# A two-row rounded pass for the rows 384 of the cosines, and a last step whose four sums end one by one

## The chip, the cores and the metric

The kernel runs on one core of one Trainium2 chip. The metric is the time of one execution on the device, in microseconds (us). Of the kernel before, three runs took 1657.99, 1658.96 and 1658.97 us; their median is 1658.96 us.

## The reference, cut to what matters

```
X = fft(fft(x, axis=1), axis=2).real          # x: 8 x 3072 x 256
h = X.reshape(24576, 256) @ w_in              # w_in: 256 x 2048
g = maximum(h, 0) + alpha * minimum(h, 0)     # alpha: 2048 values
out = g @ w_out                               # w_out: 2048 x 256
```

## The kernel before

The transform over the 256 features is multiplied into `w_in` once, so what is left for each of the 8 batches is a cosine and a sine transform over the 3072 rows. Its input is folded first: rows that meet the same cosine or sine are added or subtracted, which leaves four tiles of at most 6 x 128 rows, `fce`, `fco`, `fse` and `fso` (even and odd, cosine and sine). They are multiplied with the tables `ee`, `eo` and `er` on TensorE (PE) by `dft`, L490 to L511, and the result goes to the tile `X` as a high part (rounded to the short format float32r) and a low part (the rest).

The two matmuls of the network run in 26 blocks of up to 512 columns, with 16 steps of 128 hidden units in each, 416 steps in all. A step is a first matmul (L686 to L688, three rounded passes for each of two outputs `pq`), the activation on VectorE (DVE, L704, L712, L659), ScalarE (ACT, L716 and the high part L665) and GpSimd (POOL, the low part L667), and a second matmul (L769, twelve passes into four sums `acc`). The first matmul runs three steps ahead of the second. Each engine works in the order in which the program is written. The transforms of batch b+1 stand between the steps of batch b: `cee` (even cosines) at step 40 of the batch, and the two odd ones (`unit_odd`) at its own steps 0 and 3.

One row of the folded cosines is left over: 384, with 2688, 1152 and 1920 folded onto it. Its factors are +1 and -1 in turn. In `dft` it is a matmul of its own (`zr` on table row 4) with the tile `zres`, 128 partitions of which only partition 0 isn't zero; its dtype is float32, which PE takes as two records. It belongs to three of the eight transforms of a batch: `cee`, and the `ca` half of both odd ones. `middle` holds high and low parts of the table's middle rows; they exist from batch 1 on, and batch 0 takes its middle rows in float32.

The values of these rows are made for all batches at the start, in `rows_384` on DVE, out of `xres`. One DMA on ACT's queue writes them to `resd` in DRAM (L831). `place_rows_384` (L468, ACT's queue) and `fold_rows` (L434, SyncE's queue, SP) bring them back into partition 0. `fold_128` puts column 128's value beside them on POOL (L421).

At the start eight matmuls on `dummy` run first. The folding of batch 0 is shared: `fold_sums` on PE (L392, pieces 0, 1, 3 and 5) with a copy on ACT (L399, `xeg`) and the rest on DVE (`fold_rest`, L409 to L417), and pieces 2 and 4 on DVE alone (L383). The parts of the weights come from 64-bit words: `weights_f` on ACT (L269 to L271), `weights_b` on DVE (L276, L280), `weights_m` on POOL (L289), then PE (L320).

The DMAs complete on eight semaphores in turn. Before a DMA is issued, its queue waits until the one eight before it has landed.

At the end `evacuate` copies the four sums out (L783, L785) and writes them in two DMAs (L786).

Of the kernel before, what the change touches and what calls it, by code (L numbers as in the profile page):

```python
# [20 lines left out]
P = 128  # L21
# [63 lines left out]
def _tables():  # L85
    p = PI.reshape(3, P)
    j, i2 = np.arange(193)[None, :], np.arange(192)[None, :]

    def four(full):
        a, b = np.zeros_like(full[1]), np.zeros_like(full[1])  # L90
        a[:64], b[64:] = full[1][:64], full[1][64:]
        return np.stack([full[0], a, b, full[2]], 1)

    cee = four([_cos(p[c][:, None] * j, 768) for c in range(3)])
    see = four([_sin(p[c][:, None] * j, 768) for c in range(3)])
    ceo = four([_cos(p[c][:, None] * (2 * i2 + 1), 1536) for c in range(3)])
# [3 lines left out]
    res = np.zeros((P, 1, 193))  # L100
    res[0] = (-1.0) ** np.arange(193)
# [8 lines left out]
    out = dict(  # L110
        ee=np.concatenate([cee, res, see], 1), eo=np.concatenate([ceo, seo], 1),
        er=np.concatenate([rca, res * _cos(384, 3072), rsb], 1), feat=feat, ident=ident,
    )
    return {k: np.ascontiguousarray(v, dtype=np.float32) for k, v in out.items()}

# [18 lines left out]
def fft2_prelu_ffn(ctx: ExitStack, tc: tile.TileContext, t, outputs):  # L134
# [26 lines left out]
    zres = small.tile([P, 3, P], F32, name="zres")  # L161
# [4 lines left out]
    ee = tabs.tile([P, 9, 193], F32, name="ee")  # L166
    eo = tabs.tile([P, 8, 192], F32, name="eo")
    er = tabs.tile([P, 9, 193], F32, name="er")


    wih, wil = wts.tile([P, KF, 2, P], F32R, name="wih"), wts.tile([P, KF, 2, P], F32R, name="wil")
# [4 lines left out]
    x128 = st.tile([P, 28, NB], F32, name="x128")  # L176
    xres = st.tile([P, 4, 2, 8], F32, name="xres")

    resd = dram.tile([P, 4, 8], F32, name="resd")
    xcd = dram.tile([NB, 1544], F32, name="xcd")  # L180


# [46 lines left out]
    S.dma_start(out=ident, in_=t["ident"])  # L229
    S.dma_start(out=xres, in_=t["xres"])  # L230
    S.dma_start(out=consts, in_=t["consts"])
    load(4)

    G.memset(zres, 0.0)
    G.memset(ebias, -896.0 * 2.0**23)
    G.memset(dummy.bitcast(F32), 0.0)

# [180 lines left out]

    def fold_128(b):
        G.tensor_copy(out=fold[b, "so"][:, :, 0:1], in_=f128[:, 6:12, b:b + 1])  # L420
        G.tensor_copy(out=zres[0:1, 2, 0:1], in_=r128[0:1, b:b + 1])  # L421

    def fold_whole(i, e):
        yield from fold_piece(i, e)
# [1 line left out]

    def fold_rows(b):

        places = (zres[0:1, 0], zres[0:1, 1], zres[0:1, 2], fold[b, "se"][0:1, 3])
        places = [v.rearrange("p (c d) -> p c d", d=8) for v in places]  # L430
        for i, v in enumerate(places):
            if b == i == 0:
                continue
            nc.sync.dma_start(  # L434
                out=v, in_=resd[16 * b:16 * b + 16, i].rearrange("(o c) d -> o c d", o=1),
            )

    def turn_rows(b, nm):

# [11 lines left out]
    def rows_384():  # L451

        bufr = st.tile([P, 64, 8], F32, tag="w32", name="bufr", bufs=2)
        xe, xo, a, r = (bufr[:, 4 * i:4 * i + 4] for i in range(4))
        tt = V.tensor_tensor
        tt(out=xe, in0=xres[:, :, 0], in1=xres[:, :, 1], op=ALU.add)
        tt(out=xo, in0=xres[:, :, 0], in1=xres[:, :, 1], op=ALU.subtract)
        x2, o2 = (v.rearrange("p (j i) d -> p j i d", i=2) for v in (xe, xo))
        tt(out=a[:, 0:2], in0=x2[:, :, 0], in1=x2[:, :, 1], op=ALU.add)
        tt(out=a[:, 2:4], in0=o2[:, :, 0], in1=o2[:, :, 1], op=ALU.subtract)  # L460
        tt(out=r[:, 0], in0=a[:, 0], in1=a[:, 1], op=ALU.add)
        tt(out=r[:, 1], in0=a[:, 0], in1=a[:, 1], op=ALU.subtract)
        tt(out=r[:, 2], in0=a[:, 2], in1=a[:, 3], op=ALU.add)
        tt(out=r[:, 3], in0=a[:, 2], in1=a[:, 3], op=ALU.subtract)
        return r

    def place_rows_384():
        S.dma_start(  # L468
            out=zres[0:1, 0].rearrange("p (c d) -> p c d", d=8), in_=resd[0:16, 0].rearrange("(o c) d -> o c d", o=1),
        )  # L470


    TABS = dict(cee=(ee, 0), see=(ee, 5), ceo=(eo, 0), seo=(eo, 4), ca=(er, 0), sb=(er, 5))
    middle = {}

    def parts(key, n, rows, places):
# [13 lines left out]
    def dft(kind, v, zr, m, mid=None, bank=None):  # L490

        ps = (bank or other_bank())[0:m]
        tab, at = TABS[kind]
        n = tab.shape[-1]
        even, odd = [(v[:, 0], tab[:, at])], [(v[:, 2], tab[:, at + 3])]
        if zr is not None:
            even.append((zr, tab[:, 4]))
        if mid is None:
            even.append((v[:, 1], tab[:, at + 1]))
            odd.append((v[:, 1], tab[:, at + 2]))  # L500
        else:
            (fh, fl), (th, tl) = mid, middle[kind]
            for i, (lhsT, rhs) in enumerate(((fh, th), (fh, tl), (fl, th))):
                nc.tensor.matmul(out=_pairs(ps[:, 0:2 * n]), lhsT=lhsT, rhs=_halves(rhs), start=(i == 0), stop=False)  # L504
        for o, terms in ((0, even), (n, odd)):
            for i, (lhsT, rhs) in enumerate(terms):
                nc.tensor.matmul(  # L507
                    out=ps[:, o:o + n], lhsT=lhsT, rhs=rhs, start=(mid is None and i == 0),
                    stop=(i == len(terms) - 1 and (o > 0 or mid is None)),
                )  # L510
        return ps, n, m  # L511
# [79 lines left out]


    f128 = small.tile([P, 12, NB], F32, name="f128")
    z128 = st.tile([P, NB], F32, name="z128")

    def column_128():
        tt = V.tensor_tensor
        buf8 = st.tile([P, 64, NB], F32, tag="w32", name="buf8", bufs=2)
        a = buf8[:, 0:12].rearrange("p (c j) b -> p c j b", c=3)
        ae = buf8[:, 12:18].rearrange("p (c j) b -> p c j b", c=3)  # L600
        ao = buf8[:, 18:24].rearrange("p (c j) b -> p c j b", c=3)
        v = x128[:, 0:24].rearrange("p (c j i) b -> p c j i b", c=3, i=2)
        for c in range(3):
            tt(out=a[:, c], in0=v[:, c, :, 0], in1=v[:, c, :, 1], op=ALU.add)
            a2 = a[:, c].rearrange("p (j i) b -> p j i b", i=2)
            tt(out=ae[:, c], in0=a2[:, :, 0], in1=a2[:, :, 1], op=ALU.add)
# [9 lines left out]
        G.memset(z128, 0.0)  # L616
        tt(out=z128[0:1], in0=r[:, 0], in1=r[:, 1], op=ALU.add)
        tt(out=r128, in0=r[:, 0], in1=r[:, 1], op=ALU.subtract)

    def warm_up(n):  # L620
# [121 lines left out]
    def ffn2(s):  # L742
# [7 lines left out]
        if s < WHOLE:  # L750
# [5 lines left out]
                    )  # L756
            return
        H, L = 0, 1
        if f == KF - 1:
# [15 lines left out]
    def evacuate(g, o):  # L775
# [2 lines left out]
            outs[g] = outp.tile([P, 2, 2, w], F32, tag="o", name="o")  # L778
        v = outs[g]
        dst = outputs[g]  # L780
        for i in range(2):
            if o == 1 and (i == 1 or g < len(BLOCKS) - 1):
# [171 lines left out]


_INS = [
    "xh", "xres", "x128", "w", "consts", "ee", "eo", "er", "feat", "ident",
]


# [57 lines left out]
```

## Time and profile before

| | |
|---|---|
| runs | 1657.99, 1658.96, 1658.97 us |
| profiled execution | 1658.04 us |
| its span, first to last instruction | 1656.3 us |
| PE busy | 1635.3 us, 99% |
| DVE busy | 1495.5 us, 90% |
| POOL busy | 1326.9 us, 80% |
| ACT busy | 1133.1 us, 68% |

Shares over the whole span say little of the first 45 us, in which the kernel loads and folds, and of the last 5 us. Those two stretches, and one step in the middle, are read by themselves.

### The profile page before, as it was taken

How to read it: one execution, taken by the hardware profiler on the slowest of the kernel's cores; microseconds unless marked ns; L12 is line 12 of the kernel's file. 1: busy time of each engine (PE TensorE's matmuls, PEld its weight loads, DVE VectorE, ACT ScalarE, POOL GpSimd, SP SyncE). 2: the span in 40 equal slices, each digit the busy share in tenths (PEclk: the TensorE clock that was granted, in tenths of full speed). 3: DMA queues.
4: the chain of work that ended last, by engine and by line, in shares of the span. 5: the costliest groups of instructions: out<-in, count | busy, mean ns of one | idle time of the engine just before them, and what ended most of it. 6: DMA issues, size and time to landing. Idle time of an engine off the chain costs nothing.

```text
span 1656.3 us, 26300 instructions
## 1 busy us (share of the span) xinstructions
PE 1635.3 (99%) x8154; PEld 1464.1 (88%) x8154; DVE 1495.5 (90%) x2613; ACT 1133.1 (68%) x2095; POOL 1326.9 (80%) x1420
## 2 busy tenths in 40 slices
PE   8999999999999999999999999999999999999998
PEld 6778999888888888888888888888888888899998
DVE  7979998999889997999989998899988999889997
ACT  5866777666676666766676666766667666677675
POOL 2378998888888887889878898888887888776665
PEclk9999999999999999999999999999999999999999
DMA  6410120021000110010200101001110010000000
GB/s 240 141 56 19 45 70 20 7 71 39 33 27 20 58 52 20 33 39 33 70 1 32 51 33 58 27 7 70 39 33 26 20 45 31 1 31 25 25 20 20
DMA packets 25289, 69.93 MB, mean 42 GB/s; under 512 B 6174, under 2 KB 7486, under 8 KB 25150
## 3 DMA queue, kind: packets, MB, share of 16 engines
q1 hardware_dynamic: 24398, 67.80, 11.6%
q8 instruction: 65, 1.06, 0.3%
q14 instruction: 74, 0.61, 0.1%
q10 hardware_dynamic: 752, 0.45, 0.1%
HBM read 42.98 MB, written 25.25 MB: 41 GB/s over the span
## 4 chain that ended last, share of the span: by engine, by line
PE 92%; DVE 3%; POOL 2%; ACT 2%; issue 1%; DMA 0%; ACTq 0%; DVEq 0%; POOLq 0%
PE acc L769 55%; PE pq L686 10%; PE pq L688 9%; PE pq L687 9%; PE ps L507 3%; PE acc L753 2%; PE ps L504 2%; DVE d L712 1%; PE ps L320 1%; POOL lo L667 1%; ACT pq L716 1%; DVE d L659 1%; DVE pf L704 1%; ACT hi L665 0%; PE fold L392 0%
## 5 line engine op out<-in xcount | busy, mean ns | idle before, releaser
L667 POOL TENSOR_TENSOR lo<-d,hi 128x512 fp32r<-128x512 f32 (+2 forms) x804 | 971.9, 1226 | 242.4 <-ACT hi L665 214.8
L665 ACT ACTIVATE hi<-d 128x512 fp32r<-128x512 f32 (+2 forms) x804 | 482.6, 600 | 360.7 <-DVE d L659 282.2
L659 DVE SCALAR_TENSOR_TENSOR d<-d,sg,pq 128x512 f32<-128x512 f32 (+2 forms) x804 | 564.5, 702 | 11.8 <-ACT pq L716 11.7
L716 ACT ACTIVATE pq<-d,sga 128x512 f32<-128x512 f32 (+2 forms) x804 | 526.3, 655 | 47.9 <-DVE d L712 46.3
L712 DVE TENSOR_TENSOR d<-pf,pq 128x512 f32<-128x512 f32 (+2 forms) x832 | 529.6, 640 | 11.1 <-POOL lo L667 3.2
L769 PE MATMUL acc<-hi,woh 128*128 128x512 f32 (+2 forms) x1608 | 456.5, 365 | 1.5 <-ACT o L785 1.4
L769 PE MATMUL acc<-hi,wol 128*128 128x512 f32 (+2 forms) x1608 | 392.9, 364 | 0.0
L769 PE MATMUL acc<-lo,woh 128*128 128x512 f32 (+2 forms) x1608 | 392.9, 364 | 0.0
L704 DVE SCALAR_TENSOR_TENSOR pf<-xbc,w,pq 128x512 f32<-128x512 f32 (+2 forms) x416 | 298.2, 717 | 81.9 <-PE pq L688 75.8
L769 PEld LDWEIGHTS acc<-hi,woh 128*128 128x128 f32 x1608 | 298.0, 189 | 35.7 <-ACT o L785 4.8
L769 PEld LDWEIGHTS acc<-lo,woh 128*128 128x128 f32 x1608 | 295.3, 189 | 30.9
L769 PEld LDWEIGHTS acc<-hi,wol 128*128 128x128 f32 x1608 | 295.3, 189 | 30.8
L686 PE MATMUL pq<-X,wih 128*128 128x512 f32 (+2 forms) x832 | 313.2, 376 | 8.5 <-DVE d L659 7.7
L687 PE MATMUL pq<-X,wih 128*128 128x512 f32 (+2 forms) x832 | 302.4, 364 | 0.3 <-DVE X L590 0.3
L688 PE MATMUL pq<-X,wil 128*128 128x512 f32 (+2 forms) x832 | 302.4, 364 | 0.0
L686 PEld LDWEIGHTS pq<-X,wih 128*128 128x128 f32 x832 | 157.7, 190 | 30.7 <-PE pq L688 5.8
L688 PEld LDWEIGHTS pq<-X,wil 128*128 128x128 f32 x832 | 157.6, 189 | 15.7 <-DVE wil L337 0.3
L687 PEld LDWEIGHTS pq<-X,wih 128*128 128x128 f32 x832 | 157.8, 190 | 15.2 <-issue 0.5
L383 POOL TENSOR_TENSOR raw<-raw 128x512 f32<-128x512 f32 (+2 forms) x84 | 69.4, 827 | 0.0
L289 POOL TENSOR_TENSOR w<-we,wm 128x512 int32<-128x512 int32 x16 | 20.4, 1273 | 51.5 <-DVE wm L280 47.1
L525 DVE TENSOR_TENSOR y<-ps,os 128x193 f32<-128x193 f32 (+3 forms) x68 | 21.1, 352 | 30.9 <-ACT os L515 30.9
L785 ACT ACTIVATE o<-acc 128x512 f32<-128x512 f32 (+2 forms) x53 | 26.9, 557 | 25.6 <-PE acc L769 25.5
(160 smaller groups left out, 1069.7 us busy)
## 6 DMA issues: line engine op xcount, KB each, us to landing
raw<-in_xh SPq DMA_DIRECT2D x46, 512.0 KB
out<-o SPq DMA_DIRECT2D x36, 512.0 KB
raw<-in_w SPq DMA_DIRECT2D x15, 512.0 KB
xbc<-xcd SPq DMA_DIRECT2D x18, 256.0 KB
out<-o SPq DMA_DIRECT2D x10, 386.0 KB
out<-o SPq DMA_DIRECT2D x6, 384.0 KB
before<-in_xh SPq DMA_DIRECT2D x2, 512.0 KB
xbc<-xcd SPq DMA_DIRECT2D x5, 193.0 KB
```

The costliest lines, as they stand in the source:

```text
L383: yield size, lambda o=o, i0=i0, i1=i1, op=op: e.tensor_tensor(out=o, in0=i0, in1=i1, op=op)
L507: nc.tensor.matmul(out=ps[:, o:o + n], lhsT=lhsT, rhs=rhs, start=(mid is None and i == 0), stop=(i == len(terms) - 1 and (o > 0 or mid is ...
L659: V.scalar_tensor_tensor(out=g, in0=d, scalar=sg[:, f:f + 1], in1=ad, op0=ALU.mult, op1=ALU.max)
L665: S.activation(out=hi, in_=d, func=ACTF.Copy)
L667: G.tensor_tensor(out=lo, in0=d, in1=hi.bitcast(F32), op=ALU.subtract)
L686: nc.tensor.matmul(out=out, lhsT=wih[:, f, q], rhs=xh, start=True, stop=False)
L687: nc.tensor.matmul(out=out, lhsT=wih[:, f, q], rhs=xl, start=False, stop=False)
L688: nc.tensor.matmul(out=out, lhsT=wil[:, f, q], rhs=xh, start=False, stop=True)
L704: V.scalar_tensor_tensor(out=_pairs(pf), in0=_halves(xbc[g]), scalar=w128[:, f:f + 1], in1=_pairs(ps[0]), op0=ALU.mult, op1=ALU.add,)
L712: V.tensor_tensor(out=d, in0=pf, in1=ps[1], op=ALU.add if i else ALU.subtract)
L716: S.activation(out=ad, in_=d, func=ACTF.Copy, scale=sga[:, f:f + 1])
L769: nc.tensor.matmul(out=out, lhsT=wt[:, f, o * P:(o + 1) * P], rhs=rhs, start=(f == 0 and n[o] == 0), stop=(f == KF - 1 and n[o] == 2),)
```

## The change

For the left-over row, `rows_384` multiplies in the factor cos(pi/4) of the odd transforms, rounds the three rows on ACT to a high part, takes the low part on DVE, and writes both to DRAM tiles `resph` and `respl`, each with a second small DMA that puts column 128's value into place. `place_rows_384` loads the two as two partitions of `zst` and copies them to `zres`, now 2 partitions of float32r: on ACT for batch 0, on POOL for the others. `dft` multiplies `zres` with `res`, two rows of +1 and -1 and a zero at the end: where `middle` exists as one rounded pass of 194 columns, in batch 0 as before in float32. The tables lose their row 4. The last of the 416 steps orders its twelve passes sum by sum, and the last evacuation copies and stores each sum by itself, the fourth in two halves, on ACT's and SP's queue.

```diff
+        V.tensor_scalar(out=r[:, 1:3], in0=r[:, 1:3], scalar1=COS_384, scalar2=None, op0=ALU.mult)
+        parts = bufr[:, 16:32].bitcast(F32R).rearrange("p (k i) d -> p k i d", k=4)
+        r1 = parts[0:1, 3].rearrange("p i d -> p (i d)")
+        V.tensor_scalar(out=r128, in0=r128, scalar1=COS_384, scalar2=None, op0=ALU.mult)
+        S.activation(out=parts[:, 0, 0:3], in_=r[:, 0:3], func=ACTF.Copy)
+        V.tensor_tensor(out=parts[:, 1, 0:3], in0=r[:, 0:3], in1=parts[:, 0, 0:3].bitcast(F32), op=ALU.subtract)
+        S.activation(out=r1[:, 0:NB], in_=r128, func=ACTF.Copy)
+        V.tensor_tensor(out=r1[:, NB:2 * NB], in0=r128, in1=r1[:, 0:NB].bitcast(F32), op=ALU.subtract)
+        S.dma_start(out=resd, in_=r[:, 3])
+        for i in range(2):
+            S.dma_start(out=resp[i].rearrange("i p d -> p i d"), in_=parts[:, i, 0:3].bitcast(F32))
+            S.dma_start(
+                out=resp[i].rearrange("i (b c) d -> c i b d", c=16)[0:1, 2, :, 0], in_=r1[:, i * NB:(i + 1) * NB].bitcast(F32),
+            )
+
+    def place_rows_384(b, queue):
+        for i in range(2):
+            queue.dma_start(
+                out=zst[i:i + 1], in_=resp[i][:, 16 * b:16 * b + 16].rearrange("(o i) c d -> o i (c d)", o=1),
+            )
+        if b:
+            G.tensor_copy(out=zres, in_=zst)
+        else:
+            S.activation(out=res, in_=rst, func=ACTF.Copy)
+            S.activation(out=zres, in_=zst, func=ACTF.Copy)
...
     def dft(kind, v, zr, m, mid=None, bank=None):
-        if zr is not None:
-            even.append((zr, tab[:, 4]))
         if mid is None:
+            if zr is not None:
+                even.append((zr.bitcast(F32), res[0:zr.shape[0], 0:n].bitcast(F32)))
...
             for i, (lhsT, rhs) in enumerate(((fh, th), (fh, tl), (fl, th))):
+                if i == 2 and zr is not None:
+                    nc.tensor.matmul(out=ps[:, 0:n + 1], lhsT=zr, rhs=res, start=False, stop=False)
...
     def ffn2(s):
+        if s == NSTEP - 1:
+            for o in range(2):
+                for i in range(2):
+                    for n, (wt, part) in enumerate(((woh, H), (wol, H), (woh, L))):
...
     def evacuate(g, o):
+        if g == len(BLOCKS) - 1:
+            for i in range(2):
+                parts = [slice(0, w)] if o + i < 2 else [slice(0, w // 2), slice(w // 2, w)]
+                for k, c in enumerate(parts):
+                    if (i if len(parts) == 1 else k):
+                        V.tensor_copy(out=v[:, o, i, c], in_=acc[o, i][:, c])
+                        nc.sync.dma_start(out=dst[:, o, i, c], in_=v[:, o, i, c])
+                    else:
+                        S.activation(out=v[:, o, i, c], in_=acc[o, i][:, c], func=ACTF.Copy)
+                        S.dma_start(out=dst[:, o, i, c], in_=v[:, o, i, c])
+            return
...
-    S.dma_start(out=resd, in_=rows_384())
+    rows_384()
...
-    place_rows_384()
+    place_rows_384(0, S)
```

What ACT has in its order at the start before the change, from the copy for column 128 to the second copy of a folded piece (a name such as DMAHW0 is one of the eight semaphores of the DMAs):

```order
L610 COPY f_132<-buf_134 128x48 [waits DVE_49]
L831 DMA resd<-bufr 128x32 [waits DMAHW0_49,DVE_49]
L399 ACTIVATE xeg<-fold 128x256 [waits PE_49]
L836 DMA feat<-in_feat 128x512 [waits DMAHW2_49]
L399 ACTIVATE xeg<-fold 128x256 [waits DVE_49,PE_49,Activation_49]
```

And of the change, from the same copy to the same DMA of `feat`:

```order
L633 COPY f_136<-buf_138 128x48 [waits DVE_49]
L470 ACTIVATE bufr<-bufr 128x24 [waits DVE_49]
L472 ACTIVATE bufr<-r_97 1x8 [waits DVE_49]
L474 DMA resd<-bufr 128x8 [waits DMAHW1_49]
L476 DMA resph<-bufr 128x3x8 [waits DMAHW3_49,Activation_49]
L477 DMA resph<-bufr 8x1x1 [waits DMAHW5_49,DMAHW3_49,Activation_49]
L476 DMA respl<-bufr 128x3x8 [waits DMAHW6_49,DVE_49]
L477 DMA respl<-bufr 8x1x1 [waits DMAHW6_49,DMAHW1_49,DVE_49]
L403 ACTIVATE xeg<-fold 128x256 [waits PE_49]
L878 DMA feat<-in_feat 128x512 [waits DMAHW2_49]
```

Between the copy for column 128 and the first `xeg` there are now two more copies and four more DMAs. The DMA of `resph` completes on DMAHW3 and that of `respl` on DMAHW6; each is followed by a DMA into the same DRAM tile that waits for this semaphore.

What PE has for the even cosines (`cee`) of batch 2, before and with the change:

```order
L504 MATMUL ps<-mh 128x386
L504 MATMUL ps<-ml,mh 128x386
L504 MATMUL ps<-mh,ml 128x386
L507 MATMUL ps<-ee,fce 128x193
L507 MATMUL ps<-ee,zres 128x193
L507 MATMUL ps<-ee,fce 128x193
```

```order
L527 MATMUL ps<-mh 128x386
L527 MATMUL ps<-ml,mh 128x386
L526 MATMUL ps<-res,zres 128x194
L527 MATMUL ps<-mh,ml 128x386
L530 MATMUL ps<-ee,fce 128x193 x2
```

The matmul of `zres` moved from between the two float32 ones to between two rounded ones, and takes `res` in place of `ee`.

## Rows read from the trace of the kernel before

**Rows 1.** The chain that ended last, shares of the span by engine
```profile
PE 92%; DVE 3%; POOL 2%; ACT 2%; issue 1%; DMA 0%; ACTq 0%; DVEq 0%; POOLq 0%
```

**Rows 2.** Windows: start:end, length, busy of PE, PEld, DVE, ACT, POOL; clock, DMA, GB/s
```profile
892.09:1024.10 132.01, 132.01 (x614) 115.59 (x613) 125.28 (x201) 86.28 (x143) 115.74 (x121) 1.00 0.13 47
```

**Rows 3.** Timeline of PE in `cee` of batch 3: start, length, instruction
```profile
642.02 0.33 PE L504 MATMUL ps<-ml,mh 128*128 128x386 f32 x1
642.18 0.33 PE L504 MATMUL ps<-mh,ml 128*128 128x386 f32 x1
...
642.67 0.49 PE L507 MATMUL ps<-ee,zres 128*128 128x193 f32 x2
643.00 0.49 PE L507 MATMUL ps<-ee,fce 128*128 128x193 f32 x2
```

**Rows 4.** Timeline of PE's weight loads, 128 columns each, one behind the other
```profile
34.41 0.97 PEld L320 LDWEIGHTS ps<-w,feat 128*128 128x128 f32 x8 [0.49 <-POOL w L289]
```

**Rows 5.** Timeline of the start on DVE, ACT and their queues
```profile
7.72 0.17 DVE L247 TENSOR_SCALAR sg<-consts 128x16 f32<-128x16 f32 x1
7.84 0.34 ACTq L831 DMA_DIRECT2D resd<-bufr  x1
...
9.45 0.38 ACT L399 ACTIVATE xeg<-fold 128x256 f32<-128x256 f32 x1 [2.76 <-PE fold L392]
...
11.64 0.28 DVE L409 TENSOR_TENSOR xev<-fold,xeg 128x128 f32<-128x128 f32 x1
...
13.36 0.29 DVE L409 TENSOR_TENSOR xev<-fold,xeg 128x128 f32<-128x128 f32 x1 [0.24 <-ACT xeg L399]
...
14.35 0.57 ACTq L468 DMA_DIRECT2D zres<-resd  x1
...
19.52 0.28 DVE L409 TENSOR_TENSOR xev<-fold,xeg 128x128 f32<-128x128 f32 x1
```

**Rows 6.** Waits of SP's queue in the first 20 us: total, times, longest
```profile
SPq L196 <- DMA resd<-bufr: 4.5, 1, 4.5
```

**Rows 7.** DMA queues in 11:13.5 (q1 SP's, q10 ACT's): packets, MB, share
```profile
q1 hardware_dynamic: 205, 0.91, 90.5%
q10 hardware_dynamic: 153, 0.04, 6.8%
```

**Rows 8.** Timeline of SP's queue: a small store, and the load that waits for it
```profile
25.19 0.22 SPq L634 DMA_DIRECT2D xcd<-y  x1
...
26.30 0.35 SPq L646 DMA_DIRECT2D xbc<-xcd  x1
```

**Rows 9.** Timeline of the start on POOL: the first `weights_m`
```profile
19.68 1.27 POOL L289 TENSOR_TENSOR w<-we,wm 128x512 int32<-128x512 int32 x1 [17.98 <-DVE wm L280]
```

**Rows 10.** Windows behind PE's idle time at the start, columns as in Rows 2
```profile
29.00:30.00 1.00, 0.10 (x1) 0.00 (x0) 0.57 (x2) 1.00 (x4) 0.64 (x1) 1.00 0.00 0
...
31.00:32.00 1.00, 1.00 (x6) 1.00 (x6) 1.00 (x3) 1.00 (x3) 0.19 (x1) 0.50 0.05 0
...
33.00:34.00 1.00, 1.00 (x6) 0.92 (x4) 0.24 (x1) 1.00 (x2) 0.93 (x1) 0.69 1.03 354
```

**Rows 11.** Timeline of POOL: a fill of 384 columns, and the low parts ahead of L421
```profile
0.74 0.42 POOL L234 MEMSET zres<- 128x384 f32 x1 [0.29 <-POOLq L983]
...
628.26 2.54 POOL L667 TENSOR_TENSOR lo<-d,hi 128x512 fp32r<-128x512 f32 x2 [1.35 <-ACT hi L665]
```

**Rows 12.** Timeline of the end on ACT, SP's queue and DVE
```profile
1650.87 1.47 ACT L785 ACTIVATE o<-acc 128x386 f32<-128x386 f32 x3 [2.60 <-PE acc L769]
...
1651.77 1.20 SPq L786 DMA_DIRECT2D out<-o  x2
1652.01 0.56 DVE L783 COPY o<-acc 128x386 f32<-128x386 f32 x1 [4.38 <-PE acc L769]
```

**Rows 13.** Windows of the last store, columns as in Rows 2
```profile
1652.50:1652.75 0.25, 0.00 (x0) 0.00 (x0) 0.07 (x1) 0.00 (x0) 0.00 (x0) 1.00 0.69 272
...
1654.50:1654.75 0.25, 0.00 (x0) 0.00 (x0) 0.00 (x0) 0.00 (x0) 0.00 (x0) 1.00 0.30 111
```

More of the change, by code (lines that the diff above doesn't have):

```diff
@@ L65 @@
 _EV, _OD = np.arange(0, 384, 2), np.arange(1, 384, 2)
+COS_384 = float(np.cos(np.pi / 4))
 PI = np.concatenate([_EV[:128], _EV[128:], _OD[:64], _OD[64:]]).astype(np.int64)
@@ L99, in _tables @@
     seo = four(s)
-    res = np.zeros((P, 1, 193))
-    res[0] = (-1.0) ** np.arange(193)
     turn = _cos(p, 3072)
@@ L110, in _tables @@
     out = dict(
-        ee=np.concatenate([cee, res, see], 1), eo=np.concatenate([ceo, seo], 1),
-        er=np.concatenate([rca, res * _cos(384, 3072), rsb], 1), feat=feat, ident=ident,
+        ee=np.concatenate([cee, see], 1), eo=np.concatenate([ceo, seo], 1),
+        er=np.concatenate([rca, rsb], 1), feat=feat, ident=ident,
+        res=np.tile(np.append((-1.0) ** np.arange(193), 0.0), (2, 1)),
     )
@@ L160, in fft2_prelu_ffn @@
     ebias = small.tile([P, 1], F32, name="ebias")
-    zres = small.tile([P, 3, P], F32, name="zres")
+    zres = small.tile([2, 3, P], F32R, name="zres")
+    res = small.tile([2, 194], F32R, name="res")
+    zst = small.tile([2, 3, P], F32, name="zst")
     r128 = small.tile([1, NB], F32, name="r128")
@@ L164, in fft2_prelu_ffn @@
     dummy = work.tile([P, 512], F32R, tag="hi0", name="dummy", bufs=3)
-    ee = tabs.tile([P, 9, 193], F32, name="ee")
+    ee = tabs.tile([P, 8, 193], F32, name="ee")
     eo = tabs.tile([P, 8, 192], F32, name="eo")
-    er = tabs.tile([P, 9, 193], F32, name="er")
+    er = tabs.tile([P, 8, 193], F32, name="er")
     wih, wil = wts.tile([P, KF, 2, P], F32R, name="wih"), wts.tile([P, KF, 2, P], F32R, name="wil")
@@ L177, in fft2_prelu_ffn @@
     xres = st.tile([P, 4, 2, 8], F32, name="xres")
-    resd = dram.tile([P, 4, 8], F32, name="resd")
+    resd = dram.tile([P, 8], F32, name="resd")
+    resp = [dram.tile([3, P, 8], F32, name="resp" + h) for h in "hl"]
     xcd = dram.tile([NB, 1544], F32, name="xcd")
@@ L231, in fft2_prelu_ffn @@
     S.dma_start(out=consts, in_=t["consts"])
+    rst = before[0:2, 1, 0:194]
+    S.dma_start(out=rst, in_=t["res"])
     load(4)
-    G.memset(zres, 0.0)
     G.memset(ebias, -896.0 * 2.0**23)
@@ L420, in fold_128 @@
         G.tensor_copy(out=fold[b, "so"][:, :, 0:1], in_=f128[:, 6:12, b:b + 1])
-        G.tensor_copy(out=zres[0:1, 2, 0:1], in_=r128[0:1, b:b + 1])
     def fold_whole(i, e):
@@ L427, in fold_rows @@
     def fold_rows(b):
[L429 to L436, printed above, removed]
+        nc.sync.dma_start(
+            out=fold[b, "se"][0:1, 3].rearrange("p (c d) -> p c d", d=8),
+            in_=resd[16 * b:16 * b + 16].rearrange("(o c) d -> o c d", o=1),
+        )
+        if b:
+            place_rows_384(b, nc.sync)
     def turn_rows(b, nm):
@@ L464, in rows_384 @@
         tt(out=r[:, 3], in0=a[:, 2], in1=a[:, 3], op=ALU.subtract)
[L465 to L473, printed above, removed]
+        V.tensor_scalar(out=r[:, 1:3], in0=r[:, 1:3], scalar1=COS_384, scalar2=None, op0=ALU.mult)
[16 more added lines that the diff above has]
+                out=zst[i:i + 1], in_=resp[i][:, 16 * b:16 * b + 16].rearrange("(o i) c d -> o i (c d)", o=1),
+            )
+        if b:
+            G.tensor_copy(out=zres, in_=zst)
+        else:
+            S.activation(out=res, in_=rst, func=ACTF.Copy)
+            S.activation(out=zres, in_=zst, func=ACTF.Copy)
+    TABS = dict(cee=(ee, 0), see=(ee, 4), ceo=(eo, 0), seo=(eo, 4), ca=(er, 0), sb=(er, 4))
     middle = {}
@@ L593, in fft2_prelu_ffn @@
     f128 = small.tile([P, 12, NB], F32, name="f128")
-    z128 = st.tile([P, NB], F32, name="z128")
+    z128 = st.tile([1, NB], F32, name="z128")
     def column_128():
@@ L615, in column_128 @@
         tt(out=r, in0=v[:, :, 0], in1=v[:, :, 1], op=ALU.add)
-        G.memset(z128, 0.0)
-        tt(out=z128[0:1], in0=r[:, 0], in1=r[:, 1], op=ALU.add)
+        tt(out=z128, in0=r[:, 0], in1=r[:, 1], op=ALU.add)
         tt(out=r128, in0=r[:, 0], in1=r[:, 1], op=ALU.subtract)
@@ L758, in ffn2 @@
         H, L = 0, 1
+        if s == NSTEP - 1:
+            for o in range(2):
+                for i in range(2):
+                    for n, (wt, part) in enumerate(((woh, H), (wol, H), (woh, L))):
+                        nc.tensor.matmul(
+                            out=_pairs(acc[o, i]), lhsT=wt[:, f, o * P:(o + 1) * P], rhs=_halves(hl[i][part]),
+                            start=False, stop=(n == 2),
+                        )
+            return
         if f == KF - 1:
@@ L780, in evacuate @@
         dst = outputs[g]
+        if g == len(BLOCKS) - 1:
[8 more added lines that the diff above has]
+                        S.dma_start(out=dst[:, o, i, c], in_=v[:, o, i, c])
+            return
         for i in range(2):
-            if o == 1 and (i == 1 or g < len(BLOCKS) - 1):
+            if o == 1:
                 V.tensor_copy(out=v[:, o, i], in_=acc[o, i])
@@ L956 @@
 _INS = [
-    "xh", "xres", "x128", "w", "consts", "ee", "eo", "er", "feat", "ident",
+    "xh", "xres", "x128", "w", "consts", "ee", "eo", "er", "feat", "ident", "res",
 ]
```

## Prediction

> **What bounds the kernel now.** The chain that ended last is read first: PE carries 92% of the span [rows 1], so work taken from PE counts and work taken elsewhere counts only where PE waits. The windows come next: through the 132 us in which batch 4 runs with the folds of batch 5 beside it, PE is busy without a gap and DVE 125.3 us, 95% [rows 2]. DVE can follow a PE that is quicker by some tenths of a microsecond per batch. Last, the two ends. In the first 45 us PE's chain is not the limit: DVE folds piece after piece in program order, and PE, POOL and ACT wait for it or it for them [rows 5, 9]. In the last 5 us the sums leave the core.
>
> The sum is made on the profiled execution: 1658.04 us, of which 1656.3 is its span. The median of the runs is 0.9 us above it; I add that at the end.
>
> **Part 1: the rounded pass.** In `cee` of a middle batch the two records of `zres` start at 642.67 and the next matmul at 643.00: 0.325 us for 193 float32 columns. A rounded pass of 386 columns takes 0.16 us from start to start (642.02 to 642.18) [rows 3]. For 194 rounded columns no row exists. The nearest are: half of the 386-column pass, 0.08; the whole of it, 0.16; and weight loads of 128 columns in a row, eight in 0.97 us, of which the last is 0.19 long, so 0.11 each [rows 4]. The load for the pass behind `zres` cannot hide behind a pass shorter than itself, so I take 0.11: 0.215 us saved. It counts three times in each of batches 1 to 7 (batch 0 has no `middle` and stays in float32): 21 x 0.215 = **-4.5 us**, with 21 x 0.165 = -3.4 and 21 x 0.245 = -5.1 as ends. The ends reach to nothing if the short pass runs at the float32 rate; that is a rival below.
>
> **Part 2: the batches.** SP issues three small loads per batch for the left-over rows in place of four, the last of them in the same place, and the POOL instruction that waits for the last one stands where L421 stood. A copy of 2 x 384 on POOL has no row; L421 before, a single value, is far below, the low part of 512 columns (half of 2.54 us) far above, and the fill of 384 columns at 0.42 us is the nearest [rows 11]. Seven of them are 2.9 us of POOL. They lie beside the low parts of a step ahead: POOL idled 1.35 us just before them [rows 11], and PE didn't wait. Cost 0; without that cover 0.4 us a batch, 2.9 in all.
>
> **Part 3: the start.** Here the change adds waits. Before, ACT's queue issues the one store `resd` at 7.84, its copy `xeg` of the first folded piece runs at 9.45, and DVE takes it up at 11.64 [rows 5]. With the change ACT must, before that `xeg`, make two copies, store `resd` and the high parts, *wait until the high parts have landed* (the eight values of column 128 go into the same DRAM tile), store those and the low parts, *wait until these have landed*, and store eight values more. Queued behind on ACT: the four `xeg` and every `weights_f`. Waiting for these: DVE, at `fold_rest` of piece 0, and behind DVE everybody.
>
> How long is a landing? `resd` was issued at 7.84, and what waited for it, ACT's load of `zres`, went at 14.35 [rows 5]; SP's queue waited 4.5 us for the same landing [rows 6]. So 6.5 us, in a stretch in which loads fill the DMA engines. Its packets and those around it are seen between 11 and 13.5, 153 in 2.5 us or 61 per us, beside 205 large ones of SP's queue [rows 7]. That is one end; the other is 1.1 us, from a store of one row issued at 25.19, with nothing else under way, to the load that needs it at 26.30 [rows 8].
>
> The high parts are three pieces of 32 bytes for each of 128 partitions, 384 packets where `resd` had 128. At 61 per us the 256 extra ones would take 4.2 us; but loads run out earlier, since SP's next load of weights (the second L223 of before) now waits for the high parts too. I take 7.5 us for the first landing, between 1.1 and 6.5 + 4.2 = 10.7. The moment it lands SP lets go its weight loads, four of 0.5 MB within 2 us, and the low parts go out with them. Four such loads at the 0.36 MB per us of [rows 7] need 5.8 us. I take 5.5 us, between 1.1 and 10.7.
>
> Then: DVE's two multiplications at 0.17 behind 7.72, two short copies on ACT of a quarter microsecond each (a 256-column `xeg` takes 0.38) and `resd`'s issue of 0.34 [rows 5] put the high parts' issue at about 8.9. 8.9 + 7.5 + 0.45 (the small store's issue) + 5.5 + 0.45 = 22.8 for the first `xeg`, 23.2 for DVE's first add, against 11.64: 11.6 us late. 0.24 of that DVE waited anyway, at 13.36 [rows 5]: **+11.3 us**. DVE is busy in order from there on, so it isn't made up.
>
> ACT's second stop, for the two loads of `zst` (0.57 to issue each, as for `zres` [rows 5]), hides: DVE needs the third `xeg` 19.52 - 11.64 - 0.24 = 7.6 us after its first add, at 30.8 [rows 5], and the loads issue by 27.4 and land, at twice the 1.1 us, by 29.6. DVE's own four added instructions, about 0.9 us with their two waits for ACT, lie inside the same delay.
>
> PE then stands still for some ten microseconds, since its next work after the first folds needs POOL's words, at 19.68 before [rows 9]. In the trace of before its clock falls after it has had next to no work in 29 to 30: it is granted 0.50 of full speed, 1.2 GHz, from 31 on and is back at 2.4 GHz within the window 33 to 34 [rows 10]. Some 3 us at half speed give up 1.5 us of work: **+1.5 us**, between 0 and 3.
>
> **Part 4: the end.** Before, ACT copies two sums from 1650.87, SP issues the first store at 1651.77, and DVE's copy ends at 1652.57 [rows 12]; data flow from about 1652.6 to 1654.6, the two stores' 0.79 MB without a pause [rows 13]. With the change the first sum is whole three passes (0.16 each) earlier, its store issues near 1651.1, and the flow begins some 0.7 us earlier; but the last half-sum waits on ACT behind the issue of a store, copies at 1652.5 and is issued near 1652.9, so the flow ends near 1654.0: **-0.6 us**, between 0 and -1.0. The smaller tables and the two fills that POOL loses at the start lie beside loads that are waited for in any case: 0.
>
> **Sum:** -4.5 + 0 + 11.3 + 1.5 - 0.6 = +7.7; 1658.04 + 7.7 = 1665.7, and with the 0.9 to the median 1666.6, say **1666 us**.
>
> **Rivals.** *The small stores slip through (faster).* If ACT's packets take their turn between the loads, each landing costs the 1.1 us of [rows 8]. The first `xeg` runs at 8.9 + 1.1 + 0.45 + 1.1 + 0.45 = 12.0; DVE, itself 0.9 us late, adds at 12.5: +0.6. No stop of PE is added. -4.5 + 0.6 - 0.6 = -4.5: 1653.5, on the median's scale 1654.4. It decides wherever the two landings together take under 4 us. Against it: the 6.5 us of `resd` under the same loads [rows 5, 6]. For it: fewer loads are under way, as SP now waits for `ident`, `xres` and `res` before loads that it issued at once before. The Trainium skill has this rule ("DMA: Bandwidth & Descriptors", Queues, rings and completion order): each DMA engine goes round the queues that have work for it, a packet at a time. By that rule alone a store of eight packets per engine would be through after eight turns. The trace agrees only in part: packets of both queues do alternate between 11 and 13.5, but none of `resd` is there until more than 3 us after its issue.
>
> *Only the first landing is long.* The second store leaves just as the DMA engines have run dry, and lands in 2 us. Then `xeg` runs at 8.9 + 6.5 + 0.45 + 2 + 0.45 = 18.3, DVE at 18.7: +6.8, and with 0 to 1.5 for the clock -4.5 - 0.6 + 6.8 to 8.3 = +1.7 to +3.2: 1660.6 to 1662.1. For it: SP holds its loads for the same landing. Against it: it lets them go at that moment, and they are issued a little ahead of the low parts.
>
> *The pass isn't shorter.* If 194 rounded columns take what 193 float32 ones do, the 4.5 us don't come: 1666.6 + 4.5 = 1671. No row of a rounded pass under 384 columns speaks against it.
>
> *POOL stops at its copy.* If the loads of `zst` land late, POOL holds the low parts, PE waits, and each of seven batches loses up to a landing of 1.1 us: +7.7, 1674. Against it: the loads are issued where three stood before, and the wait that POOL shows ahead of that place is for ACT, not for a load [rows 11].
>
> **How the numbers follow.** Forecast 0.52 (landings of 10 to 17 us in two: 1663.5 to 1670.5, its own range), one landing short 0.20, the pass not shorter 0.15, slipping through 0.08, POOL's stop 0.03, the rest 0.02. The bound of what a measurement can tell is 0.2%, 3.3 us: faster is under 1655.6, slower above 1662.3. Faster: 0.07, most of slipping through. Slower: the forecast, the pass, POOL, and a little of the third case, 0.74. Same: 0.19. The range takes in the second case and the pass that isn't shorter and leaves out slipping through: 1658 to 1673.
>
> **What would show it.** Right: `xeg` of the first piece near 20 to 25 us in place of 9.45, with ACT waiting for DMA just before it; the first matmul of the network some 10 us later than before, a half-clock stretch around it; then `cee` steps in 0.2 us less, and the last store's flow ending about 2.0 us after the last pass. Wrong: a first `xeg` before 15 us, rounded `res` passes that keep the next one 0.3 us away, or PE waiting in the middle of the batches.

## The result, and the profile after

The changed kernel takes 1673.8 us (median of four runs, 1672.0 to 1675.2), the kernel before 1658.5 beside it: a ratio of 1.0094, 95% interval [1.0082, 1.0106]. It is slower, as forecast, but by 15 us instead of 8. Two single runs further down, 4453 us in "both edits" and 2141 us of the kernel before beside "the end alone", lie far off for a cause that isn't known, and the medians move by under 0.2 us without them. The profiled execution took 1672.01 us, its span is 1670.1, 13.8 us more than the span of before. Two stores of SP's queue that stand in both programs divide that difference. First before, then after (start, length, queue, line, what is stored):

```profile
280.76 0.82 SPq L786 DMA_DIRECT2D out<-o  x2
...
1607.58 1.70 SPq L786 DMA_DIRECT2D out<-o  x2
```

```profile
292.10 0.81 SPq L828 DMA_DIRECT2D out<-o  x2
...
1621.54 1.75 SPq L828 DMA_DIRECT2D out<-o  x2
```

| stretch | before, us | after, us | difference |
|---|---|---|---|
| span's start to the first of the two stores | 280.76 | 292.10 | +11.3 |
| from it to the second store | 1326.82 | 1329.44 | +2.6 |
| from it to the span's end | 48.72 | 48.56 | -0.2 |

The three add up to the 13.8. In the first stretch lies the start; in the second 20 of the 21 rounded passes, and hardly anything else that was changed; in the third the end.

The start, on ACT and its queue, where [rows 5] had `xeg` at 9.45 (a bracket is idle time ahead and what ended it):

```profile
8.32 0.41 ACTq L476 DMA_DIRECT2D resph<-bufr  x1
13.73 0.76 ACTq L477 DMA_DIRECT2D resph<-bufr  x1
14.59 0.41 ACTq L476 DMA_DIRECT2D respl<-bufr  x1
23.31 0.66 ACTq L477 DMA_DIRECT2D respl<-bufr  x1
24.02 0.39 ACT L403 ACTIVATE xeg<-fold 128x256 f32<-128x256 f32 x1 [15.91 <-DMA respl<-bufr]
```

The high parts land after 5.4 us (8.32 to 13.73), the low parts after 8.7 (14.59 to 23.31). `xeg` follows the second. SP's queue shows what leaves at the moment of the first landing, and travels beside the low parts:

```profile
13.68 0.33 SPq L226 DMA_DIRECT2D before<-in_w  x1
14.14 1.78 SPq L199 DMA_DIRECT2D raw<-in_w  x3
```

DVE takes up the first piece 12.8 us later than the 11.64 of [rows 5]:

```profile
24.43 0.29 DVE L413 TENSOR_TENSOR xev<-fold,xeg 128x128 f32<-128x128 f32 x1 [12.22 <-ACT xeg L403]
```

The network's first matmul, into `pq`, comes 13.9 us later, at 41.22 in place of 27.36. The first one into `acc`, behind a wait for POOL's words that is about as long in both programs (2.6 and 2.8 us), comes 12.8 us later, at 55.47 in place of 42.71. The windows show PE at half clock (0.50, 1.2 GHz) ahead of both (columns as in [rows 10]):

```profile
28.00:32.00 4.00, 2.84 (x8) 0.74 (x8) 3.97 (x15) 2.99 (x6) 0.00 (x0) 0.50 0.00 1
32.00:36.00 4.00, 2.35 (x10) 2.35 (x11) 3.90 (x20) 2.66 (x6) 1.27 (x1) 0.50 0.42 135
```

It has 18 matmuls to do in these 8 us and waits for others in between, and the first matmul into `acc` is as late as DVE's first add: by then the half clock has added nothing to the 12.8.

The rounded pass, in the `cee` of a middle batch, answers to [rows 3]:

```profile
654.15 0.33 PE L527 MATMUL ps<-ml,mh 128*128 128x386 f32 x1
654.40 0.35 PE L526 MATMUL ps<-res,zres 2*128 2x194 f32 x1
654.69 0.43 PE L527 MATMUL ps<-mh,ml 128*128 128x386 f32 x1
654.95 0.82 PE L530 MATMUL ps<-ee,fce 128*128 128x193 f32 x4
```

From `ml,mh` to the next float32 pass are 0.80 us. Two 386-column passes at 0.16 leave 0.48 for `res`, where the float32 pair took 0.325. The weight loads of the same place show how:

```profile
653.99 0.19 PEld L527 LDWEIGHTS ps<-ml,mh 128*128 128x128 f32 x1
654.40 0.18 PEld L526 LDWEIGHTS ps<-res,zres 2*128 2x128 f32 x1 [0.23 <-issue]
654.68 0.19 PEld L527 LDWEIGHTS ps<-mh,ml 128*128 128x128 f32 x1
```

In the middle of a batch a load normally runs ahead, during the pass in front of its own. That of `res` does not: it starts with its matmul, after 0.23 us in which PE's loader waited for nothing that is seen. The load of the next pass starts only 0.28 us after it.

The end answers to [rows 12]:

```profile
1665.62 1.90 SPq L818 DMA_DIRECT2D out<-o  x2
1665.65 0.33 PE L785 MATMUL acc<-lo,woh 128*128 128x386 f32 x1
...
1666.44 0.33 ACT L820 ACTIVATE o<-acc 128x193 f32<-128x193 f32 x1 [0.42 <-ACT o L820]
...
1666.80 0.36 DVE L817 COPY o<-acc 128x193 f32<-128x193 f32 x1 [1.21 <-ACT o L820]
```

Each of the first three sums and each half of the fourth has its own store now, but DVE's half starts 1.2 us after the engine came free: it waits for ACT's half of the same sum. From the last matmul's start to the span's end are 4.50 us; before, 1651.65 to 1656.26, they were 4.61. The last window in which data still flow is this one (columns as in [rows 13]):

```profile
1668.25:1668.50 0.25, 0.00 (x0) 0.00 (x0) 0.00 (x0) 0.00 (x0) 0.00 (x0) 0.50 0.53 164
```

The last packets end 2.84 us after that matmul's start; before, where data still flow in the window from 1654.50, they end 3.08 us after it.

### The profile page after: what moved, and what is told of

The parts are those of the page before. It is cut to its first block, busy times and chain, and to the rows that moved or that the text cites. A ratio compares the mean times of both kernels' runs of the same rounds, so it can differ in the third digit from the quotient of the medians.

```text
span 1670.1 us, 26260 instructions
## 1 busy us (share of the span) xinstructions
PE 1640.0 (98%) x8133; PEld 1459.9 (87%) x8133; DVE 1495.1 (90%) x2618; ACT 1134.6 (68%) x2099; POOL 1329.6 (80%) x1417
## 4 chain that ended last, share of the span: by engine, by line
PE 92%; issue 3%; POOL 2%; ACT 2%; DVE 1%; ACTq 0%; POOLq 0%; DVEq 0%
PE acc L800 55%; PE pq L708 10%; PE pq L710 9%; PE pq L709 9%; PE ps L530 3%; PE acc L775 2%; PE ps L527 2%; POOL lo L689 1%; PE ps L324 1%; DVE d L734 1%; PE ps L526 0%; ACT pq L738 0%; DVE d L681 0%; ACT hi L687 0%; DVE pf L726 0%
## 5 line engine op out<-in xcount | busy, mean ns | idle before, releaser
L800 PEld LDWEIGHTS acc<-hi,wol 128*128 128x128 f32 x1604 | 294.6, 189 | 30.8
```

The lines of the kernel that those rows point to most:

```text
L800: nc.tensor.matmul(out=out, lhsT=wt[:, f, o * P:(o + 1) * P], rhs=rhs, start=(f == 0 and n[o] == 0), stop=(f == KF - 1 and n[o] == 2),)
```

## The experiments

Theory A: ACT's two stops ahead of the first `xeg` are the whole loss of the start, and the rounded pass is dear because it uses two rows of the array between passes that use 128. Against it stand a start that costs by its stores and copies, and a pass that is dear by its length or its format. "Per pass" below is the time between the two stores of the table above, less that of before (1326.82 us), over 20 passes; after has +0.13. The kernel before took 1657.9 to 1658.7 us beside these runs.

**128 rows.** `zres`, `zst` and `res` get 128 partitions; rows 2 to 127 of `zst` are filled with zeros once.

```
-    zres = small.tile([2, 3, P], F32R, name="zres")
+    zres = small.tile([P, 3, P], F32R, name="zres")
```

> Against the changed kernel (1673.8 us): zres and res span all 128 partitions again (rows 0 and 1 hold the high and low parts, the rest zeros), everything else stays. Theory A (the rounded pass is dear because it uses two rows of the array among passes that use 128): the 21 res passes fall from about 0.48 us of step time to 0.11, the cee step of a middle batch from 5.51 to 5.14 us, the time by 21 x 0.37 = 7.8 to 1666. Rival B (a rounded pass of 194 columns is slow in itself): the step stays at 5.5 and the time at 1673 to 1675.

Measured: 1669.6 us. The pass does what theory A says; from `ml,mh` to the next float32 pass are now 0.44 us, and from `res` to the pass behind it 0.09:

```profile
659.16 0.33 PE L528 MATMUL ps<-ml,mh 128*128 128x386 f32 x1
659.33 0.25 PE L527 MATMUL ps<-res,zres 128*128 128x194 f32 x1
659.42 0.35 PE L528 MATMUL ps<-mh,ml 128*128 128x386 f32 x1
659.60 0.82 PE L531 MATMUL ps<-ee,fce 128*128 128x193 f32 x4
```

Between the two stores the kernel needs 1322.74 us, 6.7 less than after and 4.1 less than before: -0.20 per pass. B, a pass dear by its length, falls. But the median fell by 4 only, not by the 7.8 of theory A. In the profiled execution, the longest of its four, both landings were long, 9.2 us for the high parts and 7.7 (18.98 to 26.64) for the low ones:

```profile
8.46 0.39 ACTq L477 DMA_DIRECT2D resph<-bufr  x1
17.62 1.26 ACTq L478 DMA_DIRECT2D resph<-bufr  x1
```

Why the first took 9.2 here and 5.4 above isn't settled. This kernel loads `res` with 128 rows ahead of it; but in "two rows in float32" below, whose start is that of the changed kernel, it took 7.0 (8.41 to 15.38). A second thing that held the gain back shows up further down ("both edits").

**Stores first.** Both parts are stored before the two small stores of column 128 follow.

```
             S.dma_start(out=resp[i]..., in_=parts[:, i, 0:3].bitcast(F32))
+        for i in range(2):
             S.dma_start(
```

> Against the changed kernel (1673.8 us): the stores of the high and of the low parts are both issued before the two stores of column 128, so that their landings overlap. Theory A (the start is lost to two landings one behind the other): the first xeg comes at 15 to 17 us in place of 24.0 and the time falls by 7 to 9, to 1666. Rival B (a landing is as long as the bytes ahead of it, so two stores together take as long as one after the other): first xeg at 21 to 24, the time within 3 us of 1673.8.

Measured: 1665.8 us, as A says; the profiled execution, at 1663.1 us, was the shortest of its four. The two landings overlap; the second had come by the time the issue of the first small store was over:

```profile
8.37 0.39 ACTq L476 DMA_DIRECT2D resph<-bufr  x1
8.85 0.44 ACTq L476 DMA_DIRECT2D respl<-bufr  x1
12.80 0.77 ACTq L478 DMA_DIRECT2D resph<-bufr  x1
13.68 0.64 ACTq L478 DMA_DIRECT2D respl<-bufr  x1
14.37 0.38 ACT L403 ACTIVATE xeg<-fold 128x256 f32<-128x256 f32 x1 [6.21 <-DMA resph<-bufr]
```

**No landing ahead of `xeg`.** Column 128's parts go to a tile of their own, `c128`, on chip; POOL copies its column into `zres` after the rest, and makes batch 0's copies too.

```
-            S.dma_start(
-                out=resp[i]...[0:1, 2, :, 0], in_=r1[...].bitcast(F32),
-            )
+            S.dma_start(out=c128[i:i + 1], in_=r1[...].bitcast(F32))
...
+        G.tensor_copy(out=zres[:, 2, 0:1], in_=c128[:, b:b + 1])
```

> Against the changed kernel (1673.8 us): column 128's high and low values go into a small tile of their own and from there by a copy into zres, so nothing on ACT waits for a landing ahead of the first xeg; the copies into res and zres of batch 0 move to POOL. Theory A (the two landings are the whole loss of the start): first xeg at 10.5 to 12 us, DVE's third fold_rest at 19.5 to 21, the time falls by 11 to 13, to 1661.5. Rival B (the stores, copies and other queue waits of the start cost by themselves): first xeg above 14, the time above 1665.

Measured: 1660.8 us, ratio to before 1.0013 [1.0004, 1.0022]. All five stores are still issued by ACT, in 3 us, and `xeg` follows the last at once:

```profile
10.82 0.67 ACTq L478 DMA_DIRECT2D c<-bufr  x1
11.54 0.38 ACT L404 ACTIVATE xeg<-fold 128x256 f32<-128x256 f32 x1 [2.81 <-DVE raw L388]
```

A holds for most of the start. The first matmul into `acc` comes at 44.47, 1.8 us later than in the kernel before, where the changed kernel had 12.8. In the other seven kernels with no landing it comes between 42.72 and 45.58, 0 to 2.9 us late, so what is left differs from one execution to the next. By the first of the two marking stores, 280.46 where before has 280.76, these 1.8 us are made up as well; "both edits" shows by what. Between the stores the dear pass is left: 1329.55 us, +0.14 per pass.

**Two rows in float32.** The pass is taken back to two records of 193 float32 columns, with two rows as they are.

```
-                if i == 2 and zr is not None:
-                    nc.tensor.matmul(out=ps[:, 0:n + 1], lhsT=zr, rhs=res, start=False, stop=False)
```

> Against the changed kernel (1673.8 us): the two rows stay two rows, but go through as 193 float32 columns (two records) in all batches, where the kernel before had 128 rows in float32 at 0.325 us. Theory A (two rows among 128 cost, whatever the number format): the pass costs some 0.3 us over the 0.325 of 128 rows, as batch 0's res of the changed kernel does (0.42 before and 0.52 at it in place of two times 0.325), so 0.14 more than the rounded one: 1673.8 + 21 x 0.14 = 1676.7. Rival B (the rounded format is what costs): 0.325 as before, 21 x 0.155 less: 1670.5.

Measured: 1679.0 us, and 1334.17 between the stores: +0.37 per pass against before, where the pass has 128 rows. So two rows cost 0.33 (rounded: 0.13 + 0.20) to 0.37 (float32), and the format isn't at fault. A's sum is 2.3 us short: the float32 pass is 0.24 dearer than the rounded one with two rows, not 0.14. The two records of `res` take 0.52 us to the next pass, and those of the pass ahead 0.41 in place of 0.325:

```profile
658.72 0.49 PE L528 MATMUL ps<-ee,fce 128*128 128x193 f32 x2
659.13 0.59 PE L528 MATMUL ps<-res,zres 2*128 2x193 f32 x2
659.65 0.59 PE L528 MATMUL ps<-ee,fce 128*128 128x193 f32 x2
```

**Both edits.** 128 rows and `c128`.

> The changed kernel with both edits together: 128-row zres and res (rows 0 and 1 the parts, the rest zeros), and column 128's values through their own small tile, so that no landing stands ahead of the first xeg. Theory A (the two losses are separate and add): the time without landings, 1660.8, less 21 x 0.37 (0.09 between starts where two rows took 0.45 to 0.48) gives 1653.0, under the 1658.3 of the kernel before by about 5. Rival B (once PE is quicker, DVE, 95% busy in the middle batches, takes part of it back): 1655 to 1657, and PE waits for DVE grow.

Measured: 1655.2 us, ratio 0.9982 [0.9973, 0.9991]. The kernel beats the one before. A's sum of 1653.0 is missed by 2.2 us, though: between the stores all is there, 1322.82 us, but the first store comes at 281.96, 1.5 us later than with two rows. Counted from the first matmul into `acc`, which leaves out how the start went, it comes after 238.0 us instead of 236.0. B is right in part: PE waits 7.8 us for DVE in all (7.7 in the kernel before), and 5.4 with two rows. The place is a single DVE instruction near 126 us, an add of a fold, seen here with POOL's work beside it (the middle two rows, POOL's own add of a fold among them, directly behind two others that end at 126.77), and PE's wait behind it:

```profile
126.28 2.96 DVE L389 TENSOR_TENSOR xev<-raw 128x512 f32<-128x512 f32 x1
...
126.71 1.29 POOL L389 TENSOR_TENSOR xeg<-raw 128x512 f32<-128x512 f32 x1
...
127.94 0.74 POOL L318 TENSOR_TENSOR wol<-whole,woh 128x256 fp32r<-128x256 f32 x1
...
130.34 0.43 PE L707 MATMUL pq<-X,wih 128*128 128x384 f32 x1 [1.96 <-DVE d L680]
```

In the kernel with two rows and no landing the same add comes a few tenths of a microsecond later and takes 0.80 us, and POOL's own is the longer one, 1.72 in place of 1.29:

```profile
126.61 0.80 DVE L388 TENSOR_TENSOR xev<-raw 128x512 f32<-128x512 f32 x1
...
126.82 1.72 POOL L388 TENSOR_TENSOR xeg<-raw 128x512 f32<-128x512 f32 x1
```

**The fourth sum whole.** As the last kernel; DVE copies the fourth sum in one piece.

```
-                parts = [slice(0, w)] if o + i < 2 else [slice(0, w // 2), slice(w // 2, w)]
+                parts = [slice(0, w)]
```

> As the kernel with 128 rows and no landing, and the fourth of the last sums is copied whole by DVE instead of in halves by ACT and DVE (in the changed kernel DVE's half starts 1.2 us after its engine came free, since it waits for ACT's half). Theory A (that wait ends the kernel): the last store leaves 0.6 us earlier, 1652.4 against 1653.0, seen in the span behind the last matmul rather than in the medians. Rival B (the stores' bytes, some 2 us of transfer, set the end): the time behind the last matmul stays within 0.2 us.

Measured: 1655.1 us. The last store is issued at 1648.48, 1.0 us after the last matmul's start (1647.53), where it was 1.5. The 0.79 MB flow without a pause from 1647.8 to 1650.1; the last window with data is

```profile
1650.00:1650.25 0.25, 0.00 (x0) 0.00 (x0) 0.00 (x0) 0.00 (x0) 0.00 (x0) 1.00 0.07 19
```

The time behind that matmul is 4.40 us, against 4.65, and the last packets end 2.58 us after its start, against 2.83. That is 0.25 us: less than half of A's 0.6, and a little over B's 0.2. It is no accident of one execution: in the two kernels below that have this same end the data stop 2.58 us after the last matmul's start too, and in all ten traces with halves 2.82 to 2.84 us after it. The medians, 1655.2 and 1655.1, don't tell so small a gain from none.

**64 rows.** As "no landing", with 64 partitions in `zres` and `res`.

> Against the kernel with no landing and two rows (1660.8 us): zres and res span 64 partitions (rows 0 and 1 the parts, the rest zeros). Theory A1 (any pass that uses fewer than all rows pays): the pass and its neighbours stay at about 0.80 us from ml,mh to the next float32 matmul, the time at 1660.8. Theory A2 (only a pass of a few rows pays): 0.44 us as with 128 rows, 1653.0.

Measured: 1660.9 us, and again 0.81 us across the pass:

```profile
643.47 0.33 PE L526 MATMUL ps<-ml,mh 128*128 128x386 f32 x1
...
644.28 0.82 PE L529 MATMUL ps<-ee,fce 128*128 128x193 f32 x4
```

A2, that only a pass of a few rows is dear, falls.

**Twice.** As "no landing", each rounded `res` pass run twice.

> Against the kernel with no landing and two rows (1660.8 us): each of the 21 rounded res passes runs twice, one behind the other, so rows 384 count double in batches 1 to 7. Theory A (the price is paid at going from 128 rows to two and back): the second one adds 0.09 to 0.12 us, in all 2 to 2.5, 1663. Rival B (a pass of two rows is slow in itself): it adds 0.35 to 0.48 each, 7.4 to 10, 1668 to 1671.

Measured: 1663.0 us; between the stores 2.2 us more than with one pass, 0.11 each. From `ml,mh` to the first float32 pass are 0.92 us instead of 0.81:

```profile
643.29 0.33 PE L526 MATMUL ps<-ml,mh 128*128 128x386 f32 x1
643.55 0.46 PE L525 MATMUL ps<-res,zres 2*128 2x194 f32 x2
...
644.21 0.82 PE L529 MATMUL ps<-ee,fce 128*128 128x193 f32 x4
```

So a two-row pass behind a two-row pass costs nearly as little as one of 128 rows behind its like. The price is paid on going from 128 rows to two and back; B falls.

**96 rows.** As "no landing", with 96 partitions.

> Against the kernel with no landing, where two rows (1660.8 us) and 64 rows (1660.9) cost the same: zres and res span 96 partitions (rows 0 and 1 the parts, the rest zeros). Theory A (a pass that doesn't use the rows its neighbours use pays, whatever their number): 0.8 us from ml,mh to the next float32 matmul, 1660.8. Rival B (64 rows or fewer are one way of using the array, 96 and 128 another): 0.44 us, 1655.2 as with 128 rows.

Measured: 1656.2 us, -0.20 per pass, and 0.44 us across it:

```profile
643.70 0.33 PE L526 MATMUL ps<-ml,mh 128*128 128x386 f32 x1
...
644.14 0.82 PE L529 MATMUL ps<-ee,fce 128*128 128x193 f32 x4
```

A, in the form that any row count other than the neighbours' pays, falls too: 2 and 64 rows pay, 96 go with 128. The Trainium skill ("TensorEngine Tiling (Array Packing)", Tiling Modes and Key Properties) has the array run as whole, in halves of 64 rows or in quarters of 32, and drain when that mode changes. The four row counts measured here agree with it, if a plain matmul of up to 64 rows counts as such a part of the array, which no run here shows; of a drain the trace shows no more than the two late loads above.

**The end alone.** The kernel before with the new last step and its stores.

> The kernel before with the new end alone (the last step's sums one by one and their four stores; rows 384 as before). By the changed kernel's trace (the last data flow ends 2.5 us after the last matmul's start there, as in the kernel before, to about 0.2) theory A: the time behind the last matmul is shorter by 0.2 us and the median not to be told from 1658. Rival B, the prediction's term: 0.6 us shorter.

Measured: 1657.8 us, ratio 0.9996 [0.9987, 1.0006]; from the last matmul's start to the span's end 4.75 us (1651.40 to 1656.14), against 4.61 before. Neither 0.2 nor 0.6 is there. The data do stop earlier, 2.83 us after the last matmul's start where it was 3.08; but what follows behind the last data takes 1.5 us in the trace of before and 1.9 in this one (1.6 to 1.9 in the others), so that the 0.25 us are seen neither in this span nor in the median.

**POOL's fold later.** The kernel with the fourth sum whole; in batch 0 the first two of POOL's four folds begin one step later, and DVE's stay.

```
-        r_odd, r_fold, r_end = (16, 16, 50) if b == 0 else (0, 4, 36)
+        r_odd, r_fold, r_end = (16, 17, 50) if b == 0 else (0, 4, 36)
```

> The fastest version so far (128 rows, no landing, fourth sum whole: 1655.1 us) with the folds on POOL in batch 0 begun one step later; DVE's order stays. Its trace, and that of the kernel before, have one DVE fold add of 512 columns that takes 2.96 us in place of 0.80 near 125 us, with POOL at work without a gap beside it, and PE then waits 1.96 us for DVE; in the traces with two rows (a slower PE) it takes 0.80. Theory A (that meeting costs the 2.2 us that are missing from 1660.8 - 7.8 = 1653.0): without POOL's fold there it takes 0.7 to 0.9 us and the time falls by about 2 to 1653. Rival B (the stretched add is beside the path, or another meeting takes its place): 1655, PE still waits 2 us for DVE between 110 and 195.

Measured: **1653.3 us**, ratio to before 0.9966 [0.9952, 0.9979], the fastest. The two adds no longer meet:

```profile
126.46 1.02 DVE L389 TENSOR_TENSOR xev<-raw 128x512 f32<-128x512 f32 x1
...
128.33 1.28 POOL L389 TENSOR_TENSOR xeg<-raw 128x512 f32<-128x512 f32 x1
```

PE's longest wait for DVE between 110 and 195 us falls from 2.0 to 1.1 us, and from the first matmul into `acc` to the first marking store are 236.2 us, where the kernel with the fourth sum whole took 237.8. A holds.

**Both folds later.** The same with 18.

> As the kernel with POOL's folds of batch 0 one step later, but the folds on both engines later (POOL two steps, DVE one). Theory A: if the two adds no longer meet, 1653 as well; the stretched add is seen in the trace or not, and the time goes with it. Rival B: 1655 whether it is there or not.

Measured: 1655.2 us. Of the 16 such adds on DVE one takes 3.99 us (the median of them 0.79), in the middle of POOL's work again:

```profile
183.96 3.99 DVE L389 TENSOR_TENSOR xev<-raw 128x512 f32<-128x512 f32 x1
```

PE's longest wait for DVE is 2.7, and from the first matmul into `acc` to the first marking store are 238.7 us: another meeting took the place of the first, and the time went with it, as A says. This execution, at 1657.3 us, was the longest of eleven, with a start 2.9 us later than that of the kernel before; that the meeting is in the median one too isn't shown.

Over the twelve traces in which the folds weren't moved the longest such add goes with the row count: 2.96 to 2.98 us in before, with the end alone, with 96 and with 128 rows; 0.89 to 0.90 in after and in the five other kernels with two or 64 rows. The changed kernel thus got some 2 us back by being slower at the right place. That accounts for the 12.8 us of delay at 55 us being 11.3 at the first marking store, for the 1.8 us that the kernel with no landing made up, and for most of the 2.2 us that 128 rows fell short of theory A's sum once the landings were gone; moving POOL's folds alone gave 1.8 of them back.

## Why the prediction was right and wrong

- **Part 1 failed, and it is the miss.** The step is "for 194 rounded columns no row exists", and what followed from it: the pass was priced from 386-column passes and from weight loads, all with 128 rows, and so was each end of the range. No row of before shows a matmul that changes the number of rows, and I treated the change from 128 to 2 as free. Measured: 0.13 us dearer per pass in place of 0.215 cheaper. Over 21 passes the two are 7.3 us apart. The prediction's own sign of being wrong was there: the `res` pass keeps the next one 0.29 us away (654.40 to 654.69). The forecast for the profiled execution was 1665.7, it took 1672.0: 6.3 more, of which the pass is 7.3, the start -1.4 (11.3 in place of 11.3 + 1.5) and the end 0.4; the median lies 1.8 above that execution, not 0.9. With 128 rows the same sum comes out: 0.20 per pass, 4.2 us, inside the ends of 3.4 and 5.1. The rival "the pass isn't shorter" doubted in the right direction, but ended at nothing gained.
- **Part 2 was right.** POOL's copy takes 0.49 us (0.42 estimated), and in the middle batches no wait of PE names it.
- **Part 3: the mechanism was right, its parts were not.** Two landings in a row, SP's loads let go by the first: so it went, and "no landing" takes away 11.0 of the 12.8 us. Landings 5.4 and 8.7 us, not 7.5 and 5.5; the sum, 14.1 against 13.0, is near by luck, as the errors offset. The clock's 1.5 us is not there by the first matmul into `acc`: PE was at half speed where others set the pace. (In the trace of before the clock had fallen a little sooner than the prediction reads it: the window from 30 to 31 shows 0.60.) And "it isn't made up" is wrong by 1.5 us, by the add that was no longer held up.
- **ACT's second stop** hid as predicted: the copy of `zres` ran at 29.23, the third `xeg` behind it at 29.66, before the 30.8 at which DVE was to want it. That PE's column-128 matmul would wait for the copy of `res` (8.7 us) was not foreseen; it cost nothing, as PE had to wait for POOL's words anyway.
- **Part 4 was too hopeful.** The data stop 0.25 us earlier in place of 0.6, and the end alone shows nothing in the median. They do begin 0.7 us earlier, as forecast (0.29 us after the last matmul's start, before 0.96); the step that failed is that the end of the flow moves as much. That DVE's half would wait for ACT's was overlooked: without the halves the data stop another 0.25 us earlier.

## What to carry to other kernels

A matmul that uses few rows is not a small matmul: between passes of 128 rows it cost 0.33 to 0.37 us more than one padded with zeros to 96 or 128, so pad it, or put such passes side by side. Two values that only need to join a tile should not share a DRAM tile with a store in flight: the wait stood on an in-order queue ahead of work that had nothing to do with it. When a kernel gets faster or slower by an amount that the sum doesn't give, look for one instruction whose duration changed, before looking for many.

## What the hardware showed that was not expected

- Row counts: from the pass ahead of `res` to the float32 pass behind it 0.80 us with 2 and 64 rows, 0.44 with 96 and 128; a second two-row pass adds 0.11.
- A rounded pass of 194 columns with 128 rows is followed by the next after 0.09 to 0.10 us, under the 0.11 that I took as the floor from [rows 4].
- One DVE add of 512 columns took 2.96 us in place of 0.80, and ended about half a microsecond after the last of POOL's instructions in a row did (129.24 and 128.68 with both edits). The Trainium skill ("SBUF — State Buffer", Terms) calls the port pair that DVE and POOL share a lock held for a whole instruction; here the wait lasted through several of POOL's, which agrees with a lock that isn't handed over in between, but no run here shows the lock itself.
- A store of 384 pieces of 32 bytes landed after 5.4 and 7.0 us in two executions of the same start, after 4.4 with the stores first and after 9.2 with 128 rows. What sets it is open. Four runs with the stores first lie between 1663.1 and 1668.1 us, ten with no landing to wait for between 1659.8 and 1661.1; the runs of the other changed kernels spread by 1.3 to 4.0 us, with or without a landing, so it isn't shown that the landing makes the difference.
